# Attention with cluster routing and a gated MLP: weights by the sync queue, other query blocks, one written order

## The chip, the cores and the metric

The kernel runs on one core of a Trainium2 chip. Five engines work side by side, each on its own queue in order, and wait for one another by semaphores: TensorE (PE in the profile, with its weight loads as PEld), VectorE (DVE), ScalarE (ACT), GpSimd (POOL) and SyncE (SP), which only issues transfers. TensorE's results go to PSUM, which the kernel cuts into eight banks of 512 fp32 columns; all else lives in SBUF. The metric is the device time of one execution in microseconds, as the median of several runs.

## The reference

Four batches, eight heads, 768 positions, 64 channels a head. Each query and each key is assigned to the nearest of 16 centroids of its head; a query sees only the keys of its own cluster. The attention output of all heads, 512 channels, goes through a feed-forward layer of 2048 with a SiLU gate.

```python
q_assign = np.argmax(np.einsum('bhsd,hcd->bhsc', q_n, c_n), axis=-1)
k_assign = np.argmax(np.einsum('bhsd,hcd->bhsc', k_n, c_n), axis=-1)
mask = q_assign[:, :, :, None] == k_assign[:, :, None, :]
scores = np.where(mask, scale * np.matmul(q, k.transpose(0, 1, 3, 2)), -1000000000.0)
attn = softmax(scores)                 # exp(scores - max) / sum
x = np.matmul(attn, v)                 # then (B*S, H*D)
h = x @ w_in
out = (h / (1 + exp(-h))) @ w_out
```

## The kernel before

**Preparing a pair of heads (`part`).** Queries and keys are loaded as f32. Each is split into two f16 halves: `hi` (a scaled copy, on POOL or, in batch 0, also ACT) and `lo` (what the copy lost, on VectorE, line 440). The halves are turned so that channels lie on partitions: by one transfer through the DMA's transpose (line 453, `ab<-hl`), or in batch 0's first part on TensorE with a copy out of PSUM (`turn_pe`, `settle`). TensorE then multiplies them with the centroids (`logits`). VectorE adds the two halves' results (`total`, line 521), takes the maximum (`peak`, 532), POOL subtracts it (`below`, 535), and VectorE marks what reaches it (`mark`, 556 and 558) with 16384 for queries and, where it is missed, -16384 for keys. The marks are turned in blocks of 32 (`flip`, 565) and placed on partitions 64 to 79 under the turned halves (`put`): by four small transfers on SP (line 578, `ab<-ohT`) in most parts, by engine copies (580, 582) in batch 0's first five parts.

**Attention (`attention`).** With the marks as 16 more rows, one matmul of 80 rows gives score plus mask (line 621). The exponential runs on ScalarE (634). In batch 0 the queries are taken as a block of 256 and one of 512, in the other batches as one of 768, so that a score step fills 768 columns (512 + 256) of a two-bank PSUM tile `pS`; there are two such tiles. The values are multiplied with 65 columns, the last one for the sum (`pv`, 653), into one of four other banks `pM`; VectorE divides (`recip` 666, `norm` 671), and the result is turned by a transfer or on TensorE (`turn_x`) into `xt`.

**Feed-forward (`mlp`).** For each block of 256, 512 or 384 positions there are 16 up steps of four matmuls (730), each followed by tanh on ScalarE (736) and the gate on VectorE (741), and then down steps of sixteen matmuls for each 128 positions (759), a copy out of PSUM (772) and a store.

**Weights (`weight`).** POOL's queue issues 16 transfers (791, 795) that cast f32 to f16 on their way; a tiny copy from an exponential's result (`pace`, 789) ahead of each holds it back until then.

**What sets the order.** Each piece is a step with an engine, an estimated duration and a key. `Plan.order` plays the steps through by these estimates, gives each its buffers as they come free, and sorts the steps by their planned start; so each engine's queue has a fixed order. Loads of later batches are held to the exponentials of earlier heads (`pace`, `todo`). 60 warming matmuls on zeros stand at the lowest priority wherever TensorE would have nothing to do.

Of the kernel before, what the change touches and what calls it, by code (L numbers as in the profile page):

```python
# [10 lines left out]
f32 = mybir.dt.float32  # L11
# [4 lines left out]


class Buf:


    def __init__(self, pool):
        self.pool, self.i, self.users, self.left, self.end = pool, None, 0, 0, 0.0


class Pool:
    def __init__(self, n):
        self.free = [(0.0, i) for i in range(n)]
# [6 lines left out]
class Plan:  # L34


    LAG = {"PE": 200, "ACT": 200, "DVE": 120, "POOL": 150}

    def __init__(self):
        self.steps = []  # L40

    def step(self, eng, w, fn, after=(), use=(), key=0.0, load=None, hold=0.0, adds=None, pace=None, flip=False, lag=None, slack=0.0):
        s = Step()
        s.eng, s.w, s.fn, s.key, s.load, s.hold, s.adds, s.flip = eng, w, fn, key, load, hold, adds, flip
        s.lag = self.LAG.get(eng, 0) if lag is None else lag
        s.slack = slack
        s.use = list(use)
        s.n = len(self.steps)
        flat = []

        def gather(a):
            if isinstance(a, (list, tuple)):
                for x in a:
                    gather(x)
            elif a is not None:
                flat.append(a)

        gather(list(after))
        gather(pace)
        s.after = list({id(x): x for x in flat}.values())  # L60
        s.start = s.end = None
        for b in s.use:
            b.users += 1
            b.left += 1
        self.steps.append(s)
        return s

    def order(self):
        waits = {}
        need = {}  # L70
        engines = {}
        for s in self.steps:
            need[s.n] = len(s.after)
            for a in s.after:
                waits.setdefault(a.n, []).append(s)
            engines.setdefault(s.eng, {"t": 0.0, "ready": []})
        for s in self.steps:
            if not need[s.n]:
                engines[s.eng]["ready"].append((s.hold, s))
        wire = {"SP": 0.0, "ACT": 0.0, "POOL": 0.0}  # L80
        done = 0
        while done < len(self.steps):
            best = None
            for e in engines.values():
                for at, s in e["ready"]:
                    t = max(at, e["t"])
                    counts = {}
                    ok = True
                    for b in s.use:
                        if b.i is None:  # L90
                            counts[b.pool] = counts.get(b.pool, 0) + 1
                    for pool, k in counts.items():
                        if len(pool.free) < k:
                            ok = False
                            break
                        t = max(t, heapq.nsmallest(k, pool.free)[-1][0])
                    if not ok:
                        continue
                    cand = (t, s.key, s.n)
                    if best is None or cand[0] < best[0][0] - 1e-9 or (  # L100
                        abs(cand[0] - best[0][0]) <= 1e-9 and cand[1:] < best[0][1:]
                    ):
                        best = (cand, s, e)
            if best is None:
                left = [s for s in self.steps if s.start is None]
                raise RuntimeError("no step can go: " + ", ".join(f"{s.eng} {s.fn.__name__}" for s in left[:8]))
            (t, _, _), s, e = best
            s.start = t
            e["t"] = t + s.w
            e["ready"] = [x for x in e["ready"] if x[1] is not s]  # L110
            if s.load is not None:
                turned = s.load > 0 and s.flip
                begin = max(t + 300 if turned else t + s.w + 900, wire[s.eng])
                shared = 0.0
                for ring, until in wire.items():
                    if ring != s.eng and until > begin:
                        shared += min(until - begin, s.load)
                        wire[ring] += min(until - begin, s.load) / 2
                wire[s.eng] = begin + s.load + shared / 2
                s.end = max(wire[s.eng], t + s.w) + (1000 if turned else 1200) + s.slack  # L120
            else:
                s.end = t + s.w + s.lag
            for b in s.use:
                if b.i is None:
                    b.i = heapq.heappop(b.pool.free)[1]
                b.left -= 1
                b.end = max(b.end, s.end)
                if not b.left:
                    heapq.heappush(b.pool.free, (b.end, b.i))
            if s.adds is not None:  # L130
                pool, more = s.adds
                for i in more:
                    heapq.heappush(pool.free, (s.end, i))
            for x in waits.get(s.n, ()):
                need[x.n] -= 1
                if not need[x.n]:
                    at = x.hold
                    for a in x.after:
                        late = a.end
                        if a.eng == x.eng and a.load is None:  # L140
                            late = a.start + a.w
                        at = max(at, late)
                    engines[x.eng]["ready"].append((at, x))
            done += 1
        return sorted(self.steps, key=lambda s: (s.start, s.n))

@with_exitstack
def kernel(
# [10 lines left out]
    nc = tc.nc  # L159
# [4 lines left out]
    NT = B * S  # L164
    NJ = S // 128
    NFB = DF // 128
    NR = DM // 128
    NA = 2
    NB = NJ - NA
    MOST = 128 * max(NB, NJ // 2)  # L170
    assert D == 64 and DM == H * D and S == 768 and HC == 16 and H == 8
# [5 lines left out]
    WN = 32  # L177
    NP = H // 2
# [5 lines left out]
    def many(name, n, shape, dt):  # L184
        return [const.tile(shape, dt, name=f"{name}{i}") for i in range(n)]

# [3 lines left out]
    stk = const.tile([128, H, WN], f16, name="stk")  # L190
    half = const.tile([128, 1], f32, name="half")
    pace = const.tile([128, 1], f32, name="pace")
# [10 lines left out]
        "hl": (3, [128, 2 * (NJ + NA), 2, D], f16),  # L203
        "ab": (5, [128, 24, 128], f16),
        "vt": (10, [128, NJ * VW], f16),
        "P": (12, [128, 128 * max(NJ, 2 * NB)], f16),
        "gq": (7, [128, 4, MOST], f16),
        "xt": (3, [128, NR, S], f16),
        "xn": (3, [128, NJ, 128], f16),
        "L": (2, [128, 18, HC], f32),  # L210
        "mx": (2, [128, 18], f32),
        "Df": (2, [128, 18, HC], f32),
        "oh": (2, [128, 18, 32], f16),
        "ohT": (3, [128, 18, 32], f16),
        "tn": (3, [128, MOST], f32),
# [3 lines left out]
    T = {n: many(n, c, shape, dt) for n, (c, shape, dt) in sizes.items()}  # L219
    pools = {n: Pool(c) for n, (c, _, _) in sizes.items()}  # L220
    pS = [ps.tile([128, 1024], f32, name=f"pS{i}") for i in range(2)]
    pM = [ps.tile([128, 512], f32, name=f"pM{i}") for i in range(4)]
    banks = [*pM, pS[0][:, 0:512], pS[0][:, 512:1024], pS[1][:, 0:512], pS[1][:, 512:1024]]
    pools |= {"S": Pool(2), "M": Pool(4)}

    def buf(name):
        return Buf(pools[name])

    plan = Plan()
    step = plan.step  # L230

    def act_w(n):
        return 110 + 0.833 * n

    def dve_w(n, r=1.05, c=150):
        return c + r * n

    def pool_w(n, r=1.2):
        return 110 + r * n

    def mm_w(n):
        return n / 2.4 + 3

    SMALL = 30
    ISSUE = 450
    W_IN, W_OUT = 8, 26
    WARM = 60
    LATE = 1000


    def consts_v():
        nc.vector.memset(zeros, 0.0)
        for t in T["oh"]:
            nc.vector.memset(t, 0.0)
        nc.vector.memset(stk, 0.0)

    s_const = step("DVE", 900, consts_v, key=-100)

    def consts_p():
        nc.gpsimd.memset(half, 0.5)  # L260
        make_identity(nc, ident)

    s_ident = step("POOL", 700, consts_p, key=-100)

    def v_ones(i):
        def f():
            nc.gpsimd.memset(T["vt"][i][:, 0 : NJ * VW].rearrange("p (j c) -> p j c", c=VW)[:, :, D : D + 1], 2.0)

        return step("POOL", 130, f, key=-99 + i if i < 2 else -60 + i)
# [13 lines left out]
    for _ in range(WARM):  # L283
        last = warm(last)
# [619 lines left out]
```

## Time and profile before

| | |
|---|---|
| median of 3 runs | 348.39 us (348.15 to 349.97) |
| span of the profiled execution, first to last instruction | 341.5 us |
| what lies around it, to the median | 6.9 us |
| mean granted TensorE clock | 0.950 |
| transfers | 43.88 MB, 128 GB/s on the mean |

The profile was taken in an execution of its own, whose whole time is not shown beside its span; the median of the runs is 6.9 us over that span, and this is taken as what lies around it. A row of the windows gives, for a stretch of the span, the busy time of each engine with the count of its instructions, the clock that TensorE was granted (1.00 is full), and what the transfers did. A row of a group names the line, the engine, the operation, out<-in by the program's names with the shapes, and the count; then busy time in us and the mean of one in ns; then the idle time ahead of them and what ended it. "The chain that ended last" is followed back from the last instruction, at each step to what released it.

### The profile page before, as it was taken

The page shows a single profiled execution, that of the slowest core. Times are in us where ns is not written, and L with a number is a line of the kernel's source. Part 1 is how long each engine was busy: PE and PEld are TensorE (multiplying, and loading weights), DVE is VectorE, ACT ScalarE, POOL GpSimd, SP SyncE. Part 2 cuts the span into 40 slices and gives each one's busy share as a digit, 9 for nine tenths or more (in the row PEclk, how much of TensorE's full clock was granted, in tenths as well). Part 3 has the DMA queues.
Part 4 walks back from the last instruction along what each step waited for, and adds up shares of the span by engine and source line. Part 5 has one row for each costly group of instructions (what it writes and reads, how often), then busy time and mean ns, then how long its engine had stood idle before and what let it go on. Part 6 is the DMA issues. An engine that isn't in the chain of part 4 may idle for free.

```text
span 341.5 us, 7888 instructions
## 1 busy us (share of the span) xinstructions
PE 310.4 (91%) x3035; PEld 189.6 (56%) x3035; DVE 199.0 (58%) x467; ACT 224.3 (66%) x359; POOL 80.0 (23%) x168
## 2 busy tenths in 40 slices
PE   8779587796999999979999989999999999989995
PEld 7667454543355555546665656656765564544542
DVE  5988753445465757476975579468873163261430
ACT  4687488563299877687877878768976863351431
POOL 3723441572130233313212214223100000000000
PEclk9955999659899999999999999999999999999999
DMA  7535969999965969888274975996061200101001
GB/s 227 192 111 93 161 94 177 239 166 143 222 127 133 197 135 170 217 203 219 45 136 90 228 192 88 238 209 143 11 121 42 86 2 31 61 2 61 32 30 65
DMA packets 97174, 43.88 MB, mean 128 GB/s; under 512 B 74608, under 2 KB 94064, under 8 KB 97136
## 3 DMA queue, kind: packets, MB, share of 16 engines
q1 hardware_dynamic: 90448, 39.08, 51.6%
q0 software_dynamic: 6400, 4.20, 9.8%
q8 instruction: 24, 0.39, 0.5%
q10 hardware_dynamic: 288, 0.10, 0.1%
q14 instruction: 14, 0.11, 0.1%
HBM read 27.30 MB, written 6.29 MB: 98 GB/s over the span
## 4 chain that ended last, share of the span: by engine, by line
PE 67%; DMA 14%; DVE 6%; ACT 4%; issue 4%; SPq 3%; POOL 1%; ACTq 0%; DVEq 0%; POOLq 0%
PE pM L759 19%; PE pM L730 16%; PE pS L621 14%; DMA ab<-hl 9%; PE pM L653 8%; DMA ab<-ohT 4%; PE pS L730 4%; ACT P L634 2%; SPq L578 2%; PE pS L759 2%; PE pM L505 2%; ACT tn L736 2%; DMA nk<-in_k_dram 2%; PE pM L278 2%; DVE hl L440 1%
## 5 line engine op out<-in xcount | busy, mean ns | idle before, releaser
L634 ACT ACTIVATE P<-pS 128x768 f16<-128x768 f32 (+1 forms) x184 | 149.0, 844 | 43.8 <-PE pS L621 40.4
L621 PE MATMUL pS<-ab 80*128 80x512 f16 (+1 forms) x384 | 90.9, 347 | 8.7 <-DMA ab<-ohT 4.1
L759 PE MATMUL pM<-wout_s,gq 128*128 128x512 f16 x352 | 86.3, 384 | 0.0
L730 PE MATMUL pM<-xt,win_s 128*128 128x384 f16 (+2 forms) x428 | 81.6, 329 | 4.3 <-DMA win_s<-in_moe_w_in_dram 3.7
L741 DVE SCALAR_TENSOR_TENSOR gq<-tn,pM 128x384 f16<-128x384 f32 (+2 forms) x107 | 56.5, 547 | 33.8 <-ACT tn L736 32.6
L730 PEld LDWEIGHTS <-win_s 128*128 128x128 f16 x512 | 49.1, 97 | 42.7 <-issue 5.4
L736 ACT ACTIVATE tn<-pM 128x384 f32<-128x384 f32 (+2 forms) x107 | 51.9, 504 | 20.6 <-PE pM L730 19.6
L759 PEld LDWEIGHTS <-gq 128*128 128x128 f16 x384 | 37.3, 98 | 41.1 <-issue 2.8
L621 PEld LDWEIGHTS <-ab 80*128 80x128 f16 x384 | 35.9, 102 | 34.8 <-issue 12.5
L653 PEld LDWEIGHTS <-P 128*128 128x128 f16 x1152 | 43.9, 102 | 10.5 <-ACT P L634 3.2
L653 PE MATMUL pM<-vt,P 128*128 128x65 f16 x1116 | 45.4, 200 | 2.5 <-ACT P L634 2.1
L535 POOL TENSOR_TENSOR Df<-L,mx 128x192 f32<-128x192 f32 (+1 forms) x28 | 15.1, 541 | 81.5 <-DVE mx L532 80.2
L338 POOL CAST vt<-nv 128x384 f16<-128x384 f32 x32 | 16.6, 543 | 54.4 <-DMA nv<-in_v_dram 32.6
L666 DVE RECIPROCAL rz<-pM 128x6 f32<-128x6 f32 (+2 forms) x39 | 7.1, 182 | 35.3 <-PE pM L653 35.0
L772 ACT COPY ot<-pM 128x512 f32<-128x512 f32 x22 | 12.9, 588 | 22.1 <-PE pM L759 21.4
L741 DVE SCALAR_TENSOR_TENSOR gq<-tn,pS 128x384 f16<-128x384 f32 x21 | 11.6, 554 | 19.6 <-ACT tn L736 16.0
L521 DVE TENSOR_REDUCE L<-pM 128x192 f32<-128x384 f32 (+1 forms) x28 | 14.9, 533 | 13.9 <-PE pM L505 11.3
L440 DVE SCALAR_TENSOR_TENSOR hl<-nq,hl 128x384 f16<-128x384 f32 (+3 forms) x33 | 19.4, 587 | 5.5 <-POOL hl L436 4.4
L440 DVE SCALAR_TENSOR_TENSOR hl<-nk,hl 128x384 f16<-128x384 f32 (+1 forms) x29 | 19.4, 667 | 4.6 <-POOL hl L436 4.6
L736 ACT ACTIVATE tn<-pS 128x384 f32<-128x384 f32 x21 | 9.9, 489 | 14.4 <-DVE gq L741 8.4
L671 DVE TENSOR_TENSOR xn<-pM,rz 128x384 f16<-128x384 f32 (+2 forms) x39 | 18.5, 475 | 1.2
L565 DVE STREAM_TRANSPOSE ohT<-oh 128x384 f16<-128x384 f16 (+2 forms) x33 | 18.6, 565 | 1.0
(59 smaller groups left out, 206.8 us busy)
## 6 DMA issues: line engine op xcount, KB each, us to landing
nv<-in_v_dram SPq DMA_DIRECT2D x16, 384.0 KB, 5.2
out_dram<-ot SPq DMA_DIRECT2D x24, 256.0 KB, 2.2
nk<-in_k_dram SPq DMA_DIRECT2D x15, 384.0 KB, 4.7
nq<-in_q_dram SPq DMA_DIRECT2D x12, 384.0 KB, 4.7
win_s<-in_moe_w_in_dram POOLq DMA_DIRECT2D x8, 256.0 KB, 4.9
wout_s<-in_moe_w_out_dram POOLq DMA_DIRECT2D x8, 256.0 KB, 8.6
ab<-ohT SPq DMA_DIRECT2D x96, 12.0 KB, 1.9
nq<-in_q_dram SPq DMA_DIRECT2D x4, 256.0 KB, 3.9
```

What stands on the lines that cost most here:

```text
L338: nc.gpsimd.tensor_copy(T["vt"][y.i][:, 0 : NJ * VW].rearrange("p (j c) -> p j c", c=VW)[:, :, 0:D], T["nv"][x.i][:, h, :].rearrange("p (j ...
L440: nc.vector.scalar_tensor_tensor(out=dl, in0=src, scalar=QS, in1=dh, op0=ALU.mult, op1=ALU.subtract)
L535: (nc.gpsimd if sub == "POOL" else nc.vector).tensor_tensor(out=T["Df"][Df.i][:, 0:n, :], in0=Lv(), in1=T["mx"][mx.i][:, 0:n].unsqueeze(2) ...
L565: nc.vector.transpose(T["ohT"][ohT.i][:, 0:n, :].rearrange("p n c -> p (n c)"), T["oh"][oh.i][:, 0:n, :].rearrange("p n c -> p (n c)"),)
L621: nc.tensor.matmul(pS[sb.i][:, at : at + 128 * (c1 - c0)], ab[0:80, kt[per * s + i], :], ab[0:80, qt + c0 : qt + c1, :].rearrange("p n c - ...
L634: nc.scalar.activation(out=dst, in_=src, func=AF.Exp, bias=0.0, scale=ESC)
L653: nc.tensor.matmul(banks[O.i][:, (D + 1) * t : (D + 1) * t + nn], w, vt[:, VW * j : VW * j + nn], start=(j == 0), stop=(j == NJ - 1), skip ...
L671: nc.vector.tensor_tensor(out=T["xn"][xn.i][:, 0:nq, (h % 2) * D : (h % 2) * D + D], in0=banks[O.i][:, 0 : (D + 1) * nq].rearrange("p (t c ...
L730: nc.tensor.matmul(banks[bank.i][:, 0:n], win_s[:, r, ts(fb, 128)], T["xt"][xtb[b].i][:, r, 128 * j0 : 128 * j1], start=(r == 0), stop=(r ...
L736: nc.scalar.activation(out=T["tn"][tn.i][:, 0:n], in_=banks[bank.i][:, 0:n], func=AF.Tanh, bias=0.0, scale=1.0)
L741: nc.vector.scalar_tensor_tensor(out=T["gq"][g.i][:, fb % 4, 0:n], in0=T["tn"][tn.i][:, 0:n], scalar=1.0, in1=banks[bank.i][:, 0:n], op0=A ...
L759: nc.tensor.matmul(banks[bank.i], T["gq"][gqs[quarter].i][:, fc % 4, ts(t, 128)], wout_s[:, fc, :], start=(fc == 0), stop=(fc == NFB - 1),)
```

## The change

- **Order.** The planner is gone. `ORDER` lists all steps by number in one sequence, with groups of warming matmuls between them (a negative number: how many, and into which bank; 78 in 14 groups). `CHOICE` names the engine for a step that could run on several, `PLACES` the buffer of each tile. `Plan.emit` runs through them. The loads are no longer held to exponentials, but stand where the order puts them.
- **Weights.** 16 transfers on SP's queue bring f32 blocks of 128 x 1024 (512 KB) into the buffers that queries, keys and values use as well (`raw`, 8 of them), and 16 casts write the f16 weights: 10 on POOL, 6 on VectorE. All 16 loads stand in the order ahead of the first up step.
- **Placing the codes (`put`).** No transfers any more: every `put` is an engine copy, which also multiplies with 16384. 59 on POOL, 42 on VectorE, 31 on ScalarE. The marks are plain 0 and 1 and compare the logits with the maximum directly, so `below` goes. Keys are split with the opposite sign and get their own negated centroids, and the exponential's scale is negative.
- **Other engines' work.** Of 32 value casts 8 are on VectorE, 13 on ScalarE and 11 on POOL; of the high halves 15 are on VectorE; copies out of PSUM at the end are 13 on ScalarE and 11 on VectorE.
- **Batch 0's later queries** are turned on TensorE rather than by transfers.
- **Blocks.** Queries of batches 1 to 3 are taken as 512 and 256. A score step covers two key tiles of 512 columns, or four (then two) of 256: 128 exponentials of 1024 columns and 32 of 512 take the place of 160 of 768 and 24 of 1024. Both blocks of a head share a PSUM bank for the values (in batch 0's first part both heads of a pair do). The feed-forward blocks are 512 and 256 as well (256 and 512 in batch 0).
- **PSUM.** One pool of eight banks serves everything; a score step of 1024 columns takes two neighbours.

The core of the diff:

```diff
-    def order(self):
...
+    def emit(self, warm):
+        for b, i in zip(self.bufs, PLACES, strict=True):
+            b.i = i
+        done = set()
+        for n in ORDER:
+            if n < 0:
+                warm(-n % 100, -n // 100)
+                continue
+            s = self.steps[n]
+            assert all(a.n in done for a in s.after)
+            done.add(n)
+            s.fn(s.engs[CHOICE.get(n, 0)])
...
-        "nk": (3, [128, 2, NJ * D], f32),
-        "nq": (4, [128, 2, NJ * D], f32),
-        "nv": (2, [128, 2, NJ * D], f32),
+        "raw": (8, [128, 1024], f32),
...
-        def below():
-            (nc.gpsimd if sub == "POOL" else nc.vector).tensor_tensor(
-                out=T["Df"][Df.i][:, 0:n, :], in0=Lv(),
-                in1=T["mx"][mx.i][:, 0:n].unsqueeze(2).to_broadcast([128, n, HC]), op=ALU.subtract,
-            )
...
+            def mark(e, kind=kind, m0=m0, m1=m1):
+                (nc.vector if e == "DVE" else nc.gpsimd).tensor_tensor(
+                    out=t_(oh)[:, m0:m1, 0:HC], in0=Lv()[:, m0:m1, :],
+                    in1=t_(mx)[:, m0:m1].unsqueeze(2).to_broadcast([128, m1 - m0, HC]),
+                    op=ALU.is_ge if kind == "q" else ALU.is_lt,
+                )
...
+            def put(e, g=g):
+                copy(
+                    e, t_(A)[64 : 64 + HC, a0 : a0 + n, 32 * g : 32 * g + 32], t_(ohT)[32 * g : 32 * g + HC, 0:n, :], OHV
+                )
...
-        per = {6: 1, 4: 2, 3: 2, 2: 3}[nq]
-        skip = 512 if nq == 3 else 128 * nq
+    def units_of(nq):
+        if nq == 4:
+            return [(0, 2), (2, 4), (4, 6)]
+        return [(0, 4), (4, 6)]
...
+        for u, (i0, i1) in enumerate(units_of(nq)):
+            size = w * (i1 - i0) // 512
+            sb, P = buf("bank", size), buf("P")
...
-    def weight(kind, n, x):
...
-            nc.gpsimd.tensor_copy(pace, T["P"][held[x.n].i][:, 0:1])
...
+            nc.sync.dma_start(dst, src)
+
+        def g(e):
+            src = t_(x).rearrange("p (a c) -> p a c", a=2)
...
+        s = step("SP", ("load", 2048, 256), f, after=after, use=[x], key=key)
+        s = step("POOL/DVE/ACT", ("cast", 1024), g, after=[s], use=[x], key=key + 1)
...
+                x = attention(b, 2 * p + h, 0, 4, key, O, 0) + attention(b, 2 * p + h, 4, NJ, key + 3, O, 4)
+                done += normalize(O, [(0, NJ, h, 0, x)], xn, key)
...
-        cut = NA if b == 0 else NJ // 2
+        cut = NA if b == 0 else 4
```

More of the change, by code (lines that the diff above doesn't have):

```diff
@@ L15, with __init__ @@
 AX = mybir.AxisListType
-class Buf:
[L21 to L27, printed above, removed]
+TURN_Y = 'PE'
+ORDER = [
[85 rows of a table added]
+]
+CHOICE = {
[11 rows of a table added]
+}
+PLACES = [
[29 rows of a table added]
+]
+class Buf:
+    def __init__(self, pool, size=1):
+        self.pool, self.size, self.i = pool, size, None
 class Step:
@@ L55, in gather @@
             elif a is not None:
-                flat.append(a)
+                flat[a.n] = a
         gather(list(after))
[L59 to L64, printed above, removed]
+        s.after = list(flat.values())
         self.steps.append(s)
         return s
-    def order(self):
[L69 to L145, printed above, removed]
@@ L545, in part @@
+        s_peak = step("DVE", ("peak", 16 * n), peak, after=[top], use=[Lu, mx], key=key + 1.3)
+        marks, kinds, t = [], [], 0
         for kind, h, j0, j1 in segs:
@@ L677, in attention @@
[L677 to L685 removed]
+        pvs = [x for *_, x in parts]
+        s = step("DVE", ("recip", n), recip, after=pvs, use=[O, rz], key=-1000 + key)
@@ L748, in mlp @@
-            y = step("ACT", act_w(n), tanh, after=[x], use=[bank, tn], key=-100 + 0.001 * fb)
-            gates.append(
-                step("DVE", dve_w(n), gate, after=[x, y], use=[bank, tn, g], key=-2000 + 0.001 * fb)
-            )
+            kk = 100000 + key + fb
+            x = step(
+                "PE", ("mm", NR, n), up, after=[[x_done[b, j] for j in range(j0, j1)], w_in_done[fb // 4]], use=[y, X], key=kk
+            )
+            z = step("ACT", ("act", n), tanh, after=[x], use=[y, tn], key=-100 + 0.001 * fb)
@@ L840 @@
+            "ACT/DVE", TURN_Y == "PE", ["POOL/DVE/ACT"] * 4,
         )
```

787 lines of the change are left out of this document (353 added, 434 removed), and 125 rows, old and new, of tables (CHOICE, ORDER, PLACES).

## The prediction

> **What bounds the kernel now.** I read the head of the page first: who is busy, and for what share of the span.
>
> ```profile
> span 341.5 us, 7888 instructions
> ## 1 busy us (share of the span) xinstructions
> PE 310.4 (91%) x3035; PEld 189.6 (56%) x3035; DVE 199.0 (58%) x467; ACT 224.3 (66%) x359; POOL 80.0 (23%) x168
> ```
>
> TensorE (PE) leads, but 91% is a mean over stages with different limits. So the second view is the busy time by stretch: columns are the stretch, its length, then busy time and count of PE, PEld, DVE, ACT and POOL, the granted clock, the DMA share and GB/s.
>
> ```profile
> 0.00:45.00 45.00, 36.39 (x459) 29.41 (x460) 34.19 (x100) 29.19 (x46) 18.46 (x48) 0.81 0.68 155
> 45.00:100.00 55.00, 44.90 (x405) 25.15 (x404) 27.65 (x69) 33.52 (x47) 21.01 (x43) 0.84 1.09 162
> 100.00:190.00 90.00, 86.71 (x940) 52.43 (x939) 60.38 (x133) 69.66 (x108) 23.48 (x46) 1.00 0.74 159
> 190.00:280.00 90.00, 87.83 (x951) 55.04 (x949) 56.66 (x129) 70.45 (x116) 17.10 (x33) 1.00 0.54 125
> 280.00:341.50 61.50, 54.53 (x288) 27.58 (x286) 20.09 (x39) 21.50 (x45) 0.00 (x0) 1.00 0.10 39
> 0.00:5.00 5.00, 3.96 (x25) 3.06 (x26) 1.49 (x8) 2.00 (x4) 1.65 (x18) 1.00 0.58 155
> 5.00:10.00 5.00, 5.00 (x69) 4.60 (x67) 4.75 (x14) 2.32 (x5) 2.98 (x3) 1.00 1.01 330
> 20.00:30.00 10.00, 8.47 (x103) 7.32 (x104) 8.00 (x24) 8.24 (x12) 0.76 (x3) 0.50 0.14 29
> 60.00:75.00 15.00, 13.14 (x99) 7.40 (x100) 6.99 (x16) 8.99 (x11) 9.80 (x21) 0.56 1.23 217
> 160.00:170.00 10.00, 10.00 (x92) 6.40 (x91) 9.41 (x23) 8.51 (x18) 2.83 (x6) 1.00 0.38 104
> ```
>
> Three stages. Up to 100 us PE is idle for 8.6 + 10.1 us and its clock is 0.81 and 0.84. From 100 to 280 us it is busy for 174.5 of 180 us at clock 1.00. After 280 us, with only feed-forward work left, it is idle for 7.0 us. The clock and the idle time to be won lie in the first and the last stage. Third, the chain that ended last, for what the time is there (start, length, what):
>
> ```profile
> 37.72 5.00 DMA ab<-ohT
> ...
> 72.78 12.54 DMA ab<-hl
> ...
> 269.23 1.10 PE pM L653 x36
> ...
> 327.42 10.37 PE pM L759 x48
> ...
> 337.86 0.58 ACT ot L772
> ```
>
> In the first stage the chain waits for transfers: 5.00 us for one-hot codes, 12.54 us for transposed keys. At full clock 48 matmuls of 512 columns take 10.37 us (216 ns each) and 36 value matmuls 1.10 us (30.5 ns each). The span ends 341.5 - 337.79 = 3.7 us after the last matmul, with a copy of 0.58 us and its store.
>
> **The change part by part.** Nothing leaves TensorE. The scores keep 6 x 768 columns a head (now 6 x 512 and 6 x 256), the values their 1152 matmuls, the up matmuls their columns (512 + 256 for 384 + 384). Added: batch 0's later queries are turned on PE (32 transposes of 128 columns, 54 ns at the rate above, and 32 more small matmuls of about 30 ns: 2.7 us), and 18 more warming matmuls (256 columns, 108 ns: 1.9 us, in PE's idle time). Edits that shift work off PE:
> - exps: 128 of 1024 columns and 32 of 512 for 184. The same columns in 24 fewer instructions; ACT is at 66%, so this alone moves no end.
> - codes: 112 small transfers on SP (28 parts x 4) become engine copies: DVE 42, ACT 31, POOL 59 with those that were copies before. This takes waits like the 5.00 us out of the chain; what is late next is VectorE.
> - one-hot marks straight against the maximum: POOL's 28 subtractions go, DVE's marks stay in number.
> - weights: POOL's 16 casting transfers become 16 SP loads of 512 KB and 16 casts (POOL 10, DVE 6). All stand in the order ahead of batch 0's first up step.
> - value casts and splits: 8 + 15 on VectorE that POOL or ACT did.
> - one shared pool of 8 PSUM banks, a bank per head (per pair in batch 0's first part): cover for PE, no work.
> - one written order over all engines, and a last MLP that mixes 512 and 256 blocks, so tanh and gate of one hide behind the other.
>
> So the price falls on VectorE. Its rows (op, out<-in, count | busy, mean ns):
>
> ```profile
> L440 DVE SCALAR_TENSOR_TENSOR hl<-nk,hl 128x384 f16<-128x384 f32 x26 | 16.3, 627 | 4.6 <-POOL hl L436 4.6
> L440 DVE SCALAR_TENSOR_TENSOR hl<-nq,hl 128x384 f16<-128x384 f32 x24 | 14.5, 603 | 4.4 <-POOL hl L436 4.4
> L565 DVE STREAM_TRANSPOSE ohT<-oh 128x384 f16<-128x384 f16 x24 | 13.8, 577 | 0.7
> L521 DVE TENSOR_REDUCE L<-pM 128x192 f32<-128x384 f32 x24 | 13.3, 553 | 13.8 <-PE pM L505 11.3 <-ACT P L634 2.5
> L671 DVE TENSOR_TENSOR xn<-pM,rz 128x384 f16<-128x384 f32 x23 | 12.8, 557 | 0.7
> ...
> L741 DVE SCALAR_TENSOR_TENSOR gq<-tn,pM 128x512 f16<-128x512 f32 x16 | 10.9, 682 | 9.8 <-ACT tn L736 9.7
> L558 DVE TENSOR_SCALAR oh<-Df 128x96 f16<-128x96 f32 x26 | 9.4, 360 | 7.9 <-POOL Df L535 7.8
> L532 DVE TENSOR_REDUCE mx<-L 128x12 f32<-128x192 f32 x24 | 8.5, 352 | 0.8
> ...
> L582 DVE COPY ab<-ohT 16x512 f16<-16x512 f16 x9 | 3.7, 415 | 0.2
> ...
> L535 DVE TENSOR_TENSOR Df<-pM,mx 128x256 f32<-128x256 f32 x3 | 1.3, 421 | 0.1
> ```
>
> **The sum.** The written order fixes what VectorE does before any step. I take the place where its queue is furthest ahead of TensorE's: the scores of batch 2's last head, which wait for a code copy on VectorE. In the order, up to and with that copy, VectorE has 61 low halves (49 of 384 at 16.3/26 and 14.5/24, about 0.616; the rest by length: 38 us), 48 gates (30 of 512 at 0.68, 18 of 256 at about 0.40: 27.5), 31 transposes (17.4), 22 sums (12.2), 31 maxima (10.7), 24 normalizations and 24 reciprocals (16), 40 code copies at about 0.40 (16), 58 marks (46 of 96 at 0.26, by length from the 128x256 subtraction of 421 ns, the same operation on the same engine: 15), 11 casts, 14 high halves, 8 PSUM copies, 2 leavings and the constants at some 0.16 us plus 0.5 ns an element (about 20). Together 172.5 us. From those scores on, TensorE has, at the rates above, 101 groups of four at 512 columns (87.3), 56 of four at 256 (24.4), 31 and 3 score pairs (14.0), 66 x 6 value matmuls (12.0) and small ones (1.4): 139.1 us.
>
> So the span is the 3.5 us that VectorE is idle in the first 5 us (1.49 busy), plus 172.5/u with u its busy share up to there, plus 139.1, plus 3.7 after the last matmul, plus 1.5 for the handover from the last attention head to its MLP (about half of the 3.3 us that are idle after 280 us beside that end): 147.8 + 172.5/u. The kernel before stands at the same point at about 190 us: 87.83 + 54.53 = 142.4 us of PE work remain there, and it takes 151.5 us over them, so it loses 9.1. I allow 5.2 (3.7 + 1.5). The last stage gives 3.9 us; the rest hangs on u.
>
> What is u? Before, up to 190 us, it was (34.19 + 27.65 + 60.38)/190 = 0.64, but there VectorE waited for transfers or had nothing to do. At 5 to 10 us it was 0.95, at 160 to 170 us 0.94 with PE full and ACT at 0.85. The bounds: 1.00 gives 320.3 us, 0.85 (a little above the 0.80 of 20 to 30 us) gives 350.7. I take 0.94, from the one stretch where all three engines work at once on the changed kernel's kind of mix: 183.5 us, span 331.3. The runs shown have a median of 348.39, which is 6.9 over the profiled span; with that, 338.2.
>
> **A rule on the clock.** At 20 to 30 us the clock is 0.50 though PE is busy for 8.47 of 10 us in 103 matmuls. The Trainium skill, "TensorE: Matmul & The Clock Gate", Part 1, puts the drop to half rate down to an idle window of about 3.4 us. By that rule the 14 groups of warming matmuls, spread over the first PE steps, hold the clock and my sum stands. The row does not bear the rule out in that form: there was no gap of that size in a stretch so busy. By the row the clock may drop again; by the rates above the first up step has 21.6 us of PE work ahead of it, and half of that at half clock adds up to 10 us.
>
> **The rivals.**
> 1. *VectorE becomes the bound and stands at u = 0.85* (slower). Against the order: with a strict queue each wait for ACT, PE or a load holds all behind it. For it: marks of 96 elements take 360 ns, little less than 421 for 256, so short operations beside POOL's run long; 46 marks at 0.36 add 4.6 us. The sum: 350.7 + 6.9 = 357.6. It is slower from u under 0.883, that is where VectorE needs over 195 us for the 172.5. The Trainium skill, "SBUF — State Buffer", Who interferes with whom, says that VectorE with two SBUF inputs, or in a two-port mode, and GpSimd lock each other out; that is a reason of this kind, and this trace shows only the long marks.
> 2. *The clock drops in the first 45 us* as before: plus 10, 348, no change.
> 3. *The loads are the bound.* 14.3 MB stand ahead of the first up step; 8 raw buffers let some 4 MB of it be under way, so 10.3 MB must land. At 330 GB/s (5 to 10 us) that is 31 us, at 217 (60 to 75 us) 47, at 155 (0 to 45 us) 66, against about 45 by VectorE (by its prices 38.6 us of work stand ahead of that step: 38.6/0.94 + 3.5). Against it: the small code transfers are gone. At 155 GB/s it adds some 23 us: 361. It makes the kernel slower below about 190 GB/s.
> 4. *The order is nearly exact* and VectorE never waits: 320.3 + 6.9 = 327.
> 5. That exps and banks do nothing by themselves is in the sum already.
>
> **How the numbers follow.** My case (u from 0.90 to 0.98, 346 to 331): 0.50. Rival 4: 0.10. Rival 2: 0.09. Rival 1: 0.26. Rival 3: 0.05. Changes under 0.5% can't be told from none here. Faster 0.60, same 0.09, slower 0.31. The range goes from rival 4 (326) to just short of rival 1 at u = 0.85 (357); the likeliest case alone is 331 to 346.
>
> **What would show it.** Right: no wait of PE for code transfers; VectorE over 0.9 busy up to about 185 us and its busy total near 237 (the same prices over the whole order); PE close to full from about 100 us on, and only about 4 us lost after the last attention head. Wrong: VectorE under 0.88 with PE waiting for code copies or gates (rival 1), clock near 0.5 in the first 45 us with PE on the chain (2), PE or the casts waiting for raw loads (3), or code copies and marks that take other times than 0.40 and 0.26 us.

## The result, and the profile after

The changed kernel takes 369.0 us (median; 366.2 to 371.3) where the kernel before takes 348.7 in the same comparison: a ratio of 1.057, 95% interval 1.051 to 1.064. It is slower by 20 us; the forecast was 338 us, with a range of 326 to 357. Here and below a median is that of all executions, while a ratio and its interval compare only the executions of each kernel that lie within 1.5% of its quickest, so the two can differ by a per cent. The profiled execution of the changed kernel took 371.26 us with a span of 369.5, so only 1.8 us lie around the span.

The head of its page, and the chain that ended last by engine and by line, with the chain of before by engine as the last row:

```profile
span 369.5 us, 7895 instructions
## 1 busy us (share of the span) xinstructions
PE 317.6 (86%) x3117; PEld 191.1 (52%) x3117; DVE 220.8 (60%) x519; ACT 243.0 (66%) x368; POOL 71.4 (19%) x134
...
PE 56%; DVE 21%; ACT 10%; DMA 6%; issue 5%; POOL 1%; ACTq 0%; DVEq 0%; POOLq 0%
PE p L730 20%; PE p L703 17%; PE p L602 9%; DVE gq L712 7%; PE p L619 7%; ACT tn L709 6%; DMA ab<-hl 5%; DVE hl L446 3%; ACT P L609 2%; DVE xn L655 2%; DVE ohT L555 1%; PE p L500 1%; DVE ab L300 1%; DVE oh L541 1%; DMA craw<-in_centroids_dram 1%
```

```profile
PE 67%; DMA 14%; DVE 6%; ACT 4%; issue 4%; SPq 3%; POOL 1%; ACTq 0%; DVEq 0%; POOLq 0%
```

The transfers on the chain are down from 14% to 6%, and those for codes are gone from it: that part went as meant. In their place stand the gates (DVE gq) and the tanh (ACT tn) of the feed-forward layer, and no engine is full: TensorE has lost five points, VectorE is at 60%. Where it was lost is in the busy time by stretch, in the same columns as in the prediction:

```profile
0.00:45.00 45.00, 33.97 (x461) 27.21 (x462) 33.82 (x82) 27.70 (x40) 17.62 (x37) 0.89 0.82 262
45.00:100.00 55.00, 48.01 (x585) 30.57 (x582) 44.36 (x117) 46.52 (x67) 27.07 (x48) 1.00 0.92 224
100.00:190.00 90.00, 77.18 (x818) 44.47 (x815) 67.92 (x160) 70.92 (x105) 21.40 (x39) 0.96 0.73 161
190.00:280.00 90.00, 80.92 (x704) 47.41 (x703) 46.81 (x107) 62.90 (x101) 5.29 (x10) 1.00 0.14 37
280.00:341.50 61.50, 53.38 (x446) 30.17 (x444) 19.72 (x41) 29.60 (x48) 0.00 (x0) 1.00 0.12 36
341.50:369.50 28.00, 24.10 (x119) 11.29 (x117) 8.22 (x14) 5.36 (x11) 0.00 (x0) 1.00 0.15 57
```

From 100 to 280 us TensorE is now busy for 158.1 of 180 us, where it was 174.5. Neither other engine is near full there (VectorE 114.7, ScalarE 133.8 of 180), the clock is 0.96 to 1.00, and after 190 us hardly any transfer is left. All three engines wait, then, and for each other. TensorE's own waits (us in total, times, longest) name whom:

```profile
PE p L703 <- DVE gq L712: 11.9, 17, 1.9
PE p L703 <- ACT tn L709: 3.7, 5, 1.0
...
PE p L619 <- ACT P L609: 2.2, 5, 0.7
PE p L500 <- DMA ab<-hl: 2.1, 2, 1.3
```

L703 is an up matmul (the lines of this kernel have other numbers than those of before). It needs weights and x, and from a gate or a tanh nothing but an empty PSUM bank. So the up step waits for a bank. Which bank, the timeline shows (start, length, what, and in brackets the idle time before and what ended it):

```profile
319.66 3.19 PE L703 MATMUL p<-xt,win_s 128*128 128x512 f16 x16 [0.58 <-DVE gq L712]
...
321.64 0.60 ACT L709 ACTIVATE tn<-p 128x512 f32<-128x512 f32 x1 [1.28 <-PE p L703]
322.27 0.69 DVE L712 SCALAR_TENSOR_TENSOR gq<-tn,p 128x512 f16<-128x512 f32 x1 [1.45 <-ACT tn L709]
322.99 1.36 ACT L709 ACTIVATE tn<-p 128x512 f32<-128x512 f32 x3 [0.76 <-DVE gq L712]
323.62 1.78 DVE L712 SCALAR_TENSOR_TENSOR gq<-tn,p 128x512 f16<-128x512 f32 x3 [0.66 <-ACT tn L709]
324.37 1.35 PE L703 MATMUL p<-xt,win_s 128*128 128x512 f16 x7 [1.52 <-DVE gq L712]
```

Beside it stands the written order with its places: steps 1666 (up, bank 2), 1660 (up, bank 3), 1667 and 1668 (tanh and gate of bank 2), 1661 and 1662 (tanh and gate of bank 3), 1726 (up, bank 1), 1657 (up, bank 2 anew); the sixteen matmuls from 319.66 us on are the ups on banks 2, 3, 0 and 1. The tanh of bank 2 starts at 321.64, when the up of bank 3 is through. The tanh of bank 3 starts at 322.99, when the gate of bank 2 is through (322.27 + 0.69). The up on bank 2 starts at 324.37, when the first gate of the next three is through, and that is the gate of bank 3 (323.62 + 0.69 = 324.31); its own bank had been read out at 322.96. None of the three has any data from what it waits for. What they share is the tile: banks 2 and 3 are the two halves of one PSUM tile of 1024 columns. In the kernel after all eight banks are such halves:

```
+    pairs = [ps.tile([128, 1024], f32, name=f"p{i}") for i in range(4)]
+    banks = [pairs[i // 2][:, 512 * (i % 2) : 512 * (i % 2) + 512] for i in range(8)]
```

The kernel before has four banks that are tiles of their own (pM) and two wide tiles (pS) whose halves serve as banks only at the end. So the theory was: the program's waits go by tile, eight banks cut from four tiles are in effect four, and the two halves of each take turns. I call it "pairs". The rivals: "VectorE" (the forecast's bound), "order" (a written order that doesn't fit the chip's durations) and "blocks" (512 and 256 columns).

### The profile page after: what moved, and what is told of

Read it like the earlier page. It is cut to its first block, busy times and chain, and to the rows that moved or that the text cites. A ratio compares the mean times of both kernels' runs of the same rounds, so it can differ in the third digit from the quotient of the medians.

```text
span 369.5 us, 7895 instructions
## 1 busy us (share of the span) xinstructions
PE 317.6 (86%) x3117; PEld 191.1 (52%) x3117; DVE 220.8 (60%) x519; ACT 243.0 (66%) x368; POOL 71.4 (19%) x134
## 4 chain that ended last, share of the span: by engine, by line
PE 56%; DVE 21%; ACT 10%; DMA 6%; issue 5%; POOL 1%; ACTq 0%; DVEq 0%; POOLq 0%
PE p L730 20%; PE p L703 17%; PE p L602 9%; DVE gq L712 7%; PE p L619 7%; ACT tn L709 6%; DMA ab<-hl 5%; DVE hl L446 3%; ACT P L609 2%; DVE xn L655 2%; DVE ohT L555 1%; PE p L500 1%; DVE ab L300 1%; DVE oh L541 1%; DMA craw<-in_centroids_dram 1%
## 5 line engine op out<-in xcount | busy, mean ns | idle before, releaser
L609 ACT ACTIVATE P<-p 128x1024 f16<-128x1024 f32 (+1 forms) x160 | 145.1, 939 | 32.9 <-PE p L602 23.9
L703 PE MATMUL p<-xt,win_s 128*128 128x512 f16 (+1 forms) x512 | 96.3, 327 | 19.0 <-DVE gq L712 11.9
L712 DVE SCALAR_TENSOR_TENSOR gq<-tn,p 128x256 f16<-128x256 f32 (+1 forms) x128 | 67.5, 551 | 65.6 <-ACT tn L709 49.2
L730 PE MATMUL p<-wout_s,gq 128*128 128x512 f16 x384 | 94.1, 383 | 2.8 <-ACT tn L709 1.1
L709 ACT ACTIVATE tn<-p 128x256 f32<-128x256 f32 (+1 forms) x128 | 59.0, 490 | 51.1 <-PE p L703 28.5
L602 PE MATMUL p<-ab 80*128 80x512 f16 (+1 forms) x384 | 86.3, 335 | 6.5 <-DVE ab L300 1.7
L703 PEld LDWEIGHTS <-win_s 128*128 128x128 f16 x512 | 48.6, 97 | 57.0 <-issue 26.0
L619 PEld LDWEIGHTS <-P 128*128 128x128 f16 x1152 | 47.4, 99 | 23.6 <-issue 11.3
L619 PE MATMUL p<-vt,P 128*128 128x65 f16 x1152 | 51.5, 195 | 8.3 <-ACT P L609 2.2
L302 POOL TENSOR_SCALAR ab<-ohT 16x384 f16<-16x384 f16 (+2 forms) x59 | 31.7, 538 | 113.7 <-DVE ohT L555 90.6
L446 DVE SCALAR_TENSOR_TENSOR hl<-raw,hl 128x384 f16<-128x384 f32 (+4 forms) x62 | 39.3, 654 | 2.5 <-POOL hl L302 2.0
L302 POOL TENSOR_SCALAR hl<-raw 128x384 f16<-128x384 f32 (+3 forms) x36 | 20.9, 588 | 46.3 <-DMA ab<-hl 34.9
L655 DVE TENSOR_TENSOR xn<-p,rz 128x384 f16<-128x384 f32 (+1 forms) x36 | 18.4, 512 | 5.4 <-PE p L703 2.5
```

The source lines that it names most:

```text
L302: nc.gpsimd.tensor_scalar(out=dst, in0=src, scalar1=scale, scalar2=1.0, op0=ALU.mult, op1=ALU.mult)
L446: (nc.vector if e == "DVE" else nc.gpsimd).scalar_tensor_tensor(out=dl, in0=src, scalar=scale, in1=dh, op0=ALU.mult, op1=ALU.subtract)
L602: nc.tensor.matmul(o[:, w * (i - i0) : w * (i - i0 + 1)], t_(A)[0:80, kt[i], :], rhs, start=True, stop=True)
L609: nc.scalar.activation(out=t_(P)[:, 0:n], in_=o[:, 0:n], func=AF.Exp, bias=0.0, scale=-ESC)
L619: nc.tensor.matmul(bank(O)[:, D1 * (o0 + t) : D1 * (o0 + t + 1)], t_(P)[:, w * i + 128 * t : w * i + 128 * (t + 1)], t_(vb)[:, VW * j : VW ...
L655: nc.vector.tensor_tensor(out=x, in0=o, in1=z, op=ALU.mult)
```

## The experiments

**Eight tiles.** The order, the engines and the places stay; the tiles are single, and so an exp of 1024 columns has to be two.

```
-    pairs = [ps.tile([128, 1024], f32, name=f"p{i}") for i in range(4)]
-    banks = [pairs[i // 2][:, 512 * (i % 2) : 512 * (i % 2) + 512] for i in range(8)]
+    banks = [ps.tile([128, 512], f32, name=f"p{i}") for i in range(8)]
...
+                for c in range(0, w * (i1 - i0), 512):
+                    nc.scalar.activation(
+                        out=t_(P)[:, c : c + 512], in_=banks[sb.i + c // 512], func=AF.Exp, bias=0.0, scale=-ESC
+                    )
```

> The kernel after, its order, engines and buffer places untouched, but with eight PSUM tiles of 512 columns in place of four of 1024; an exp of 1024 columns becomes two of 512. Theory 'pairs' (in the kernel after an instruction on one half of a 1024-column PSUM tile waits for the last instruction on the other half, though it needs nothing of it): most of the 37 us for which TensorE stands before a bank in the trace of after goes, less what the split exps cost; 335 to 352 us, and 'PE p <- DVE gq' falls from 11.9 us to under 4. Theory 'VectorE' (the copies and casts it took over delay the rest), theory 'order' (the written order does not fit the durations of the chip) and theory 'blocks' (blocks of 512 and 256 cost of themselves): nothing of theirs is changed, so 366 to 376 us.

Measured: 330.3 us (329.8 to 333.4), 0.959 of before (0.951 to 0.967), even below what "pairs" expected. Its page, and the wait for gates:

```profile
span 330.4 us, 8031 instructions
...
PE 306.0 (93%) x3117; PEld 187.3 (57%) x3117; DVE 218.0 (66%) x519; ACT 247.2 (75%) x496; POOL 70.7 (21%) x134
```

```profile
PE p L700 <- DVE gq L709: 0.6, 2, 0.3
```

The gates' 11.9 us are 0.6. And here are the same eight steps of the written order in this kernel:

```profile
285.76 5.47 PE L700 MATMUL p<-xt,win_s 128*128 128x256 f16 x31
...
287.37 0.60 ACT L706 ACTIVATE tn<-p 128x512 f32<-128x512 f32 x1 [0.48 <-DVE gq L709]
288.00 0.69 DVE L709 SCALAR_TENSOR_TENSOR gq<-tn,p 128x512 f16<-128x512 f32 x1 [0.65 <-ACT tn L706]
288.24 0.60 ACT L706 ACTIVATE tn<-p 128x512 f32<-128x512 f32 x1 [0.27 <-PE p L700]
288.87 0.69 DVE L709 SCALAR_TENSOR_TENSOR gq<-tn,p 128x512 f16<-128x512 f32 x1 [0.18 <-ACT tn L706]
```

TensorE runs on without a break, and the second tanh (288.24) starts while the first gate (288.00 to 288.69) is still at work. By the single matmuls of these rows, it was 5.73 us from step 1666 to the end of step 1657 (319.66 to 325.39) and is 4.05 (286.31 to 290.36).

**The control: the exps split, the pairs kept.** The edit is shown against the kernel with eight tiles.

```
-    banks = [ps.tile([128, 512], f32, name=f"p{i}") for i in range(8)]
+    pairs = [ps.tile([128, 1024], f32, name=f"p{i}") for i in range(4)]
+    banks = [pairs[i // 2][:, 512 * (i % 2) : 512 * (i % 2) + 512] for i in range(8)]
```

> The control of the run with eight tiles: the exps of 1024 columns are split in two of 512 in the same way, but the four tiles of 1024 columns stay. It costs ScalarE 128 x (2 x 0.494 - 0.921) = 8.6 us of busy time. All theories: between the time of after and 8 us above it, 366 to 377 us. If instead this run comes near the one with eight tiles, the wide exp is what costs and not the shared tile.

Measured: 367.7 us (366.8 to 374.7), 1.067 of before (1.057 to 1.077), and the wait for gates is there as in the kernel after:

```profile
PE p L704 <- DVE gq L713: 11.8, 16, 1.9
```

So splitting the exps neither costs nor brings anything that can be told, and the shared tiles alone cost 367.7 - 330.3 = 37.4 us. The steps, their order and the eight banks are the same in both runs; what differs is which banks the program takes for one tile. The waits end with semaphore events, which speaks for waits that the program sets; no run separates this from something in PSUM itself.

**Half of it.** Again against the kernel with eight tiles:

```
-    banks = [ps.tile([128, 512], f32, name=f"p{i}") for i in range(8)]
+    pairs = [ps.tile([128, 1024], f32, name=f"p{i}") for i in range(2)]
+    banks = [pairs[i // 2][:, 512 * (i % 2) : 512 * (i % 2) + 512] for i in range(4)]
+    banks += [ps.tile([128, 512], f32, name=f"s{i}") for i in range(4)]
```

> The kernel with eight PSUM tiles (330.3 us), with banks 0 to 3 made halves of two tiles of 1024 columns again; banks 4 to 7 stay tiles of their own. Order, engines, places and the split exps are the same. Theory 'pairs': a part of the 37 us between the control (367.7) and the eight tiles comes back, in the measure in which banks 0 to 3 are used: 340 to 358 us. A theory in which something else about eight tiles made that kernel fast gives 329 to 333 us.

Measured: 348.7 us (347.5 to 351.3), 1.003 of before (0.999 to 1.007). The up steps' wait for gates is half as long, and it is on the paired banks (p), hardly on the single ones (s):

```profile
PE p L702 <- DVE gq L711: 5.9, 5, 1.9
...
PE s L702 <- DVE gq L711: 0.5, 2, 0.3
```

Two pairs cost 18.4 us, four 37.4: about 9 us for each. (This run was taken at another time than the other two; the kernel before stood at 349.2 us beside it and at 348.5 beside them.)

**The same fault put into the kernel before.** Its four single banks become halves of two tiles; nothing else is touched.

```
-    pM = [ps.tile([128, 512], f32, name=f"pM{i}") for i in range(4)]
+    pW = [ps.tile([128, 1024], f32, name=f"pW{i}") for i in range(2)]
+    pM = [pW[i // 2][:, 512 * (i % 2) : 512 * (i % 2) + 512] for i in range(4)]
```

> The kernel before with one change: its four PSUM tiles of 512 columns become the halves of two tiles of 1024. No instruction is moved or added. Theory 'pairs': the same false waits arise in the kernel before, 355 to 370 us. The other theories: 347 to 350 us, as before.

Measured: 380.6 us; no interval is given for this run, but its four times lie between 374.5 and 381.3, those of before between 343.1 and 349.5. By the medians it is 32 us slower than before, by the quickest executions 31, and it is 10 us beyond what "pairs" expected. TensorE's waits in the kernel before, and then in this one:

```profile
PE pS L730 <- ACT tn L736: 3.1, 4, 0.8
...
PE pM L730 <- DVE gq L741: 0.6, 1, 0.6
```

```profile
PE pW L731 <- DVE gq L742: 7.4, 12, 1.8
...
PE pW L654 <- DVE gq L742: 4.0, 6, 0.8
...
PE pW L760 <- DVE gq L742: 3.1, 4, 1.2
```

The up steps' wait on single banks grows from 0.6 to 7.4 us, and value matmuls (L654) and down matmuls (L760) now wait for gates as well. The same cause taken away, halved and put into another kernel, each time with its price, settles "pairs" as the cause.

**VectorE, with the pairs and without.** 34 code copies go from VectorE to GpSimd, first in the kernel after, then in the one with eight tiles; the order stays.

```
     def emit(self, warm):
+        for s in self.steps:
+            if s.fn.__name__ == "put" and s.engs[0] == "POOL" and CHOICE.get(s.n, 0) == 1:
+                CHOICE[s.n] = 0
```

> The kernel after with the 34 code copies that the written choices give to VectorE, where GpSimd may do them, handed to GpSimd: 34 x 0.266 = 9 us of work leave VectorE and 34 x 0.47 = 16 us come to GpSimd, which is busy 71 of 369 us. Theory 'VectorE': 358 to 364 us. Theory 'pairs': TensorE waits for gates and exps on the wrong half, not for VectorE's load, so 366 to 372 us.

Measured: 373.3 us (369.3 to 374.4), 1.082 of before (1.067 to 1.097): just above what "pairs" expected.

> The kernel with eight PSUM tiles (330.3 us), with the same 34 code copies handed from VectorE to GpSimd as in the run that did so on the kernel after. With the false waits gone, does VectorE set the pace now? Theory 'VectorE' (as in the forecast, the attention's end goes by VectorE's work over its busy share, so 9 us less work is worth about 9 us): 319 to 324 us. Theory 'TensorE' (it is busy 306 of the 330.4 us, so nothing off it is worth more than a part of the 24 us left): 327 to 334 us.

Measured: 335.1 us (332.7 to 338.0), 0.960 of before (0.952 to 0.968): a little above what either theory expected. Relieving VectorE of 9 us in this way helps neither kernel. Why it even costs some 4 us both times, TensorE's largest wait in the second run says:

```profile
PE p L601 <- POOL ab L301: 8.6, 9, 1.6
```

In the run with eight tiles alone that wait was 1.3 us. The scores now wait for code copies on GpSimd, so these two runs can't tell what less work on VectorE alone is worth. That VectorE's load is not what made the changed kernel slow is shown by the eight tiles, where the same work stays on it and 37 us go.

**The blocks.** One line in the kernel before:

```
-        cut = NA if b == 0 else NJ // 2
+        cut = NA if b == 0 else 4
```

> The kernel before, with the last layer's query blocks of batches 1 to 3 of 512 and 256 columns in place of 384 and 384; its planner lays out the rest. Theory 'blocks' (the two sizes cost of themselves): 352 us or more. Theory 'pairs' (the sizes cost nothing; the wait on the other half does): 345 to 350 us.

Measured: 345.6 us (336.3 to 348.6), no interval given; before lies at 348.3 (346.9 to 350.3). Blocks of 512 and 256 columns don't cost anything that can be seen here.

**What gains.** The kernel with eight tiles is 18 us faster than the one before by the medians, 14 by the ratio. Two parts of the change that could have done it were taken alone. First the codes, in the kernel before:

```
-    def part(..., sub="POOL", place="DMA", code_eng=None, pace=None):
+    def part(..., sub="POOL", place="ENG", code_eng=("DVE", "ACT", "POOL", "ACT"), pace=None):
```

> The kernel before with one part of the change: the codes of all parts are copied by engines (VectorE, ScalarE, GpSimd, ScalarE for the four quarters) in place of 112 small transfers; the rest and the planner stay. TensorE waits 4.1 us for these transfers in the trace of before, and the chain that ended last has one of 5.00 us. Theory 'codes' (this part is what the kernel with eight tiles gains in its first 100 us): 333 to 343 us. Theory 'loads' (the gain there is the weights' way): 344 to 352 us.

Measured: 336.8 us (332.5 to 338.3), 0.971 of before (0.964 to 0.979). Then the weights' way, undone in the kernel with eight tiles (with `g`, the cast, left empty; the lines for the output weights are shown):

```
-            nc.sync.dma_start(dst, src)
+                nc.gpsimd.dma_start(
+                    wout_s[:, 2 * n : 2 * n + 2, :],
+                    moe_w_out[256 * n : 256 * n + 256, :].rearrange("(c p) d -> p c d", p=128),
+                )
```

> The kernel with eight PSUM tiles (330.3 us), with the weights loaded as in the kernel before, by casting transfers from GpSimd's queue straight into place, at the same places of the order; the 16 casts on VectorE and GpSimd are gone, and the 16 loads leave the sync queue. Theory 'loads' (the weights by the sync queue are what gains in the first 100 us): 337 to 350 us. Theory 'codes' (the weights' way is not what gains): 326 to 334 us.

Measured: 332.0 us (330.8 to 332.5), 0.956 of before (0.950 to 0.961). The weights by the sync queue are worth nothing here that can be told. The codes copied by engines, with the planner's new layout around them, are worth 11 us by the medians (10 by the ratio), the largest part of the gain; what makes up the rest was not taken apart. And the gain of the codes is not one of the clock over these 100 us. The first two stages of that run:

```profile
0.00:45.00 45.00, 38.99 (x434) 30.70 (x435) 33.62 (x97) 30.20 (x45) 19.56 (x49) 0.66 0.69 152
45.00:100.00 55.00, 47.73 (x520) 29.08 (x519) 34.80 (x87) 45.55 (x72) 27.09 (x55) 0.94 1.11 199
```

The clock of the first stage is lower than before (0.66 for 0.81), that of the second higher (0.94 for 0.84); over both it is 0.81 for 0.83. The first stage has 434 matmuls for 459, the second, where the chain of before waited for keys, 520 for 405.

**A new order.** With eight tiles TensorE is idle for 24 us of 330.4. Is that the order? Every step was laid out anew, each unit of scores on one bank:

```
-            return [(0, 2), (2, 4), (4, 6)]
-        return [(0, 4), (4, 6)]
+            return [(i, i + 1) for i in range(6)]
+        return [(0, 2), (2, 4), (4, 6)]
...
-        "P": (13, [128, 1024], f16),
+        "P": (26, [128, 512], f16),
```

> Eight PSUM tiles, and every step written in a new order, with engines and buffers chosen anew for the durations that the trace with eight tiles shows; each block of scores takes one bank and each exp 512 columns, and the same arithmetic is done. Theory 'order' (the 24 us for which TensorE is not busy with eight tiles come from an order that was made for other durations): 300 to 316 us. Theory 'floor' (those 24 us are the start, the loads and the end, which no order removes): 325 to 333 us.

Measured: 330.6 us (330.0 to 331.4), 0.950 of before (0.945 to 0.954): no gain over eight tiles, as "floor" had it. But the busy times between 100 and 190 us, for eight tiles and then for this order, show another reason than a floor:

```profile
100.00:190.00 90.00, 82.70 (x861) 47.44 (x860) 73.85 (x172) 78.17 (x154) 21.39 (x40) 0.96 0.69 147
```

```profile
100.00:190.00 90.00, 80.33 (x1026) 50.19 (x1025) 86.61 (x204) 74.48 (x147) 26.59 (x50) 1.00 0.76 159
```

The new order had TensorE ahead up to 100 us and then ran into VectorE, which is full (86.6 of 90). It had more code copies, and they had become dearer: 50 of 384 columns at 408 ns, where the kernel with eight tiles has 29 at 317, while the gates of 512 columns kept their 0.68 us. Of the 11.3 us between the two rows some 4.5 are the price and the rest the number. A second order was made with these prices.

```profile
L296 DVE TENSOR_SCALAR ab<-ohT 16x384 f16<-16x384 f16 x29 | 9.1, 317 | 0.8
```

```profile
L320 DVE TENSOR_SCALAR ab<-ohT 16x384 f16<-16x384 f16 x50 | 20.4, 408 | 1.0
```

> Eight PSUM tiles and a new order once more, worked out with longer durations for the VectorE instructions that read and write SBUF alone, as the first new order's trace shows them while GpSimd works (a code copy 0.48 in place of 0.27 us, a subtraction 0.68 in place of 0.47). In the first new order VectorE was busy 86.6 of 90 us between 100 and 190 us, and TensorE 80.3. Theory 'VectorE slowed by GpSimd': with more code copies on GpSimd and the rest laid out for the longer durations, 312 to 322 us. Theory 'floor' (no order gains on 330): 326 to 334 us.

Measured: 323.7 us (323.4 to 325.2), 0.926 of before (0.921 to 0.931), between the two expectations: 6.6 us were the order's, with its choice of engines and buffers. In the same 90 us TensorE is now busy for 85.9:

```profile
100.00:190.00 90.00, 85.87 (x1094) 54.07 (x1091) 85.83 (x197) 81.90 (x164) 40.94 (x72) 1.00 0.81 168
```

This version beats both kernels: 25 us under before, 45 under after. Its TensorE is busy for 94% of a span of 322.0 us.

## Why the prediction was wrong

The prediction was wrong by one step: "one shared pool of 8 PSUM banks, a bank per head: cover for PE, no work", which the sum took at nothing, and the fifth rival with it. It looked at what the pool holds and not at how it is cut. The cut costs 37 us; without it, the other errors come to 8 us on balance (338.2 forecast, 330.3 measured), in part because they cancel.

How well the rest of the sum describes the kernel without that fault can be checked, because the place it argued from, the scores of batch 2's last head, can be found in the traces. With eight tiles these scores start at 188.4 us, in the kernel after at 206.5; the forecast's 3.5 + 172.5/0.94 was 187.0. The busy time before and behind that place, eight tiles first:

```profile
0.00:188.40 188.40, 167.78 (x2007) 107.14 (x2008) 157.75 (x390) 162.10 (x319) 69.14 (x131) 0.98 0.84 208
188.40:326.70 138.30, 138.21 (x1116) 80.19 (x1112) 60.21 (x129) 84.50 (x177) 1.52 (x3) 1.00 0.14 43
```

```profile
0.00:206.50 206.50, 174.99 (x2007) 110.91 (x2008) 160.51 (x390) 159.31 (x231) 69.86 (x131) 0.96 0.76 190
206.50:365.70 159.20, 142.54 (x1116) 80.21 (x1112) 60.34 (x129) 83.08 (x137) 1.52 (x3) 1.00 0.13 38
```

- *TensorE's remaining work, 139.1 us*: right, 138.2 with eight tiles. The matmul rates of the trace of before carried over to a kernel with other blocks. In the kernel after the same 1116 matmuls take 159.2 us, so 21 of the 39 us between the two spans lie behind that place and 18 ahead of it.
- *The handover, 1.5 us*: with eight tiles TensorE loses 0.1 us there.
- *VectorE's work, 172.5 us, and its busy share, 0.94*: both wrong, and they cancel. VectorE's 390 instructions up to that place keep it busy for 157.75 us. Their single durations add up to 173.8, so the prices were right in sum (the low halves took more than was put, the code copies 0.31 us for 0.40, the marks of 96 0.27 for 0.26). But the sum multiplied counts by the mean durations of single instructions, and neighbours on VectorE overlap in time: 14.8 us too much. The share was 157.75/(188.4 - 3.5) = 0.85 with eight tiles, not 0.94. So 187.0 us came out by luck. Nor does that place move with VectorE's work: in the run that undid the weights' way, VectorE is busy for 153.2 us up to it, 4.5 less, and no copy was moved to GpSimd in exchange; the scores start at 187.7 us, 0.7 earlier, where the forecast's rule has about 5. With the share of 0.85 that rival 1 took and the work priced rightly, the span would have come out at 147.8 + 157.75/0.85 = 333.4, nearly as forecast. In the kernel after the share is 160.51/(206.5 - 3.5) = 0.79, low enough for rival 1, but it is low because VectorE waits in the ring of up, tanh and gate.
- *What lies around the span, 6.9 us*: wrong, it is about 2 us (371.26 - 369.5 in the kernel after, 332.3 - 330.4 with eight tiles). The profiled execution of before was a quick one: its span is 341.5 us, and in the runs of before that stood beside the eight tiles it was 341.2 to 347.6. With 1.9 the forecast would have been 333.
- *No waits for code transfers*: right, and worth 10 to 11 us alone. *The exps move no end*: the control, which splits them anew, agrees. *The last MLP with mixed blocks*: the blocks are harmless; in the kernel after the last stage is bad because of the pairs.
- *Rival 2, the clock*: it stood at 0.89 and 1.00 in the first two stages (0.81 and 0.84 before); whether the warming matmuls did that was not tried. *Rival 3, the loads*: 262 GB/s in the first 45 us and no wait of TensorE for a weight among the large ones; undoing the weights' way changed nothing. *Rival 4, the order nearly exact and VectorE never waiting, 327 us*: near to what eight tiles give, but VectorE stands still there for 15% of the time up to that place, so the number is near by luck; another order gave less still.

No rival named what happened. The trace of before held a hint that the prediction didn't use: at its end, where the halves of the wide tiles serve as banks, TensorE waits 3.1 us for tanh on them (the first of the two rows of before above). That this was the same fault was not tried; but a look at it, and at the two lines of the diff that make all eight banks such halves, would have raised the question.

## What to carry to other kernels

Count PSUM buffers as the program's waits see them. In these kernels two banks cut out of one tile behave as one buffer with two halves that take turns, and such a pair cost 9 us in one kernel and 16 in the other (32 us for two), of some 350. Where TensorE waits for an engine from which it needs no data, ask which buffer is being waited for, and write down the buffer's number on both sides: the wait on the wrong half is seen in a single window of the timeline. And don't price work on an engine as count times mean duration where instructions run back to back: take busy time from a window.

## What was not expected of the hardware

VectorE's instructions get longer while GpSimd works, but not all. In the second new order, VectorE's rows and then GpSimd's (whose lengths are rough):

```profile
120.94 0.52 DVE L466 SCALAR_TENSOR_TENSOR hl<-raw,hl 128x384 f16<-128x384 f32 x1
...
122.54 0.83 DVE L466 SCALAR_TENSOR_TENSOR hl<-raw,hl 128x384 f16<-128x384 f32 x1
...
125.83 0.52 DVE L466 SCALAR_TENSOR_TENSOR hl<-raw,hl 128x384 f16<-128x384 f32 x1
```

```profile
122.46 1.28 POOL L318 CAST vt<-raw 128x384 f16<-128x384 f32 x2
126.09 1.20 POOL L322 TENSOR_SCALAR ab<-ohT 16x384 f16<-16x384 f16 x2 [2.34 <-PE p L621]
```

The same subtraction takes 0.52 us where GpSimd is idle as it starts, and 0.83 where GpSimd's cast is at work already. Six traces (the kernel after, eight tiles, the control, the two runs with moved copies, the first new order) give the mean distance from one start to the next, where VectorE idles for no more than 0.02 us: the subtraction of 384 takes 0.47 us (111 cases) with GpSimd idle and 0.67 (58 cases) with GpSimd busy for over 70% of it, a code copy 0.25 (13) and 0.48 (26), but a gate of 512 columns, with one input in SBUF and one in PSUM, 0.60 (171) and 0.60 (45). The Trainium skill, "SBUF — State Buffer", Who interferes with whom, has VectorE with two SBUF inputs, or in a two-port mode, lock out GpSimd and be locked out by it, and one with a single SBUF input outside such modes left alone. The subtraction, with two inputs in SBUF, and the gate agree; the code copy has a single input and agrees if it runs in such a mode, which no trace here tells. The Trainium skill, "Perfetto Trace Analysis", Optimizing Scalar/DVE Operations, says that moving work between these two might not help, and the runs with 34 copies moved agree in what came of it: about 4 us slower both times, with TensorE waiting for GpSimd's copies. In the prediction this was the reason behind rival 1; it is real, and it is a part of what filled VectorE in the first new order, but it isn't what made the changed kernel slow.
